# Windowed attention, forward and backward: mixing the tokens before the weight products, with two more DMA transposes and all loads on GpSimd

## Chip, cores, metric

One core of one Trainium2 chip. The metric is the device time of one execution in microseconds (us), lower is better.

## The reference, cut to what matters

The image is 256 x 256 tokens with C = 384 channels, in bf16. It is cut into 1024 windows of 8 x 8 = 64 tokens. The outputs are the forward result and the gradients for x, wqkv and wo.

```python
qkv = xw @ wqkv                       # xw: windows x 64 x 384
q, k, v = qkv[..., :C], qkv[..., C:2*C], qkv[..., 2*C:]
p = softmax(einsum('bqc,bkc->bqk', q, k) * C**-0.5)
o = einsum('bqk,bkc->bqc', p, v) @ wo
# out_0 = o; out_1, out_2, out_3 = gradients of x, wqkv, wo for a given grad_out
```

Both kernels fold the weights first: A = scale * Wq Wk^T and B = Wv Wo, with their transposes. With x the tokens of a window, g its grad_out, P the probabilities and dS the gradient of the scores:

- forward: P (x B), which equals (P x) B;
- gradient of x: dS (x A^T), which equals (dS x) A^T, plus dS^T (x A) and P^T (g B^T);
- weight gradients: x^T (dS x), and x^T (P^T g), which equals (P x)^T g.

The change rests on the equalities.

## The kernel before

The unit of work is a quad: four tiles of 128 tokens, each tile two windows. There are 128 quads, and one pass of the loop over them is called a step here. An eviction, below, copies a finished product out of PSUM, where PE leaves it. Work of three neighbouring quads is interleaved in a step: `a` is the next quad, `b` the current one, `c` the one before. Comments are mine.

```python
def load(st):                                        # three steps ahead
    for t in range(QUAD):
        nc.sync.dma_start(out=xq[:, t, :], in_=dram_tile(x, bp, t0 + t))            # SP
        nc.gpsimd.dma_start(out=dq[:, t, :], in_=dram_tile(grad_out, bp, t0 + t))   # GpSimd
def load_turn(st):                                   # tokens x channels -> channels x tokens
    for src, dst in ((dq, dT), (xq, xT)):
        nc.sync.dma_start_transpose(out=dst..., in_=src...)      # 12 blocks of 128x128 each
def to_tokens(st):                                   # the projections y = xA, z = gB^T turned back
    nc.sync.dma_start_transpose(out=tok..., in_=st["yz"]...)     # 24 blocks
def uv(st, t, part):                                 # u = x B (part 0), v = x A^T (part 1)
    for m in range(CK):                              # CK = 3
        nc.tensor.matmul(pj[:], lhsT=st["xT"][:, t, m, :], rhs=wgt[:, m, :], ...)
    cp(out=dst[:, t, :], in_=pj[:])                  # ACT, 8 of them a step
def store(dst, src, bp, t):                          # two DMAs of 64 tokens
    for h, w in ((LO, 1), (HI, 0)):
        nc.gpsimd.dma_start(out=dram_tile(dst, bp, t)[WIN * w:WIN * (w + 1)], in_=src[h, :])
def attend(st, pair, after=None):                    # 64x64 quarters of the PE array
    for t in pair:
        both((pu, "ST", "xq", True), (po, "PT", "uq", True))     # dS x,   P u
        ...                                                      # evict po -> store, pu -> Uq
        both((pw, "Pb", "dq", True), (pd, "ST", "vq", False))    # P^T g,  dS v
        ...                                                      # evict pw -> Wq
    ...                                              # close dx with tok, evict, store
# [...] in a step: scores(b), softmax(b) between the uv(b), project(a), weight gradients,
# attend(c, (2, 3)), attend(b, (0, 1)), to_tokens(a)
```

## Time and profile before

| | before |
|---|---|
| median of the first 3 runs | 2078.6 us (2078.22 to 2078.69) |
| PE (TensorE) busy | 2057.4 us, 99% of the span |
| DVE, ACT, POOL (GpSimd) busy | 67%, 71%, 68% |
| moved by DMA | 409.06 MB, mean 197 GB/s |

The page of before. After the busy times come two rows by 40 slices of the span in tenths (the clock that PE was granted, as a share of full speed, and the busy share of the DMA engines), then what the DMA queues moved (q1 is SP's queue, q0 GpSimd's; packets, MB, share of 16 engines' time), then the chain of waits that ended last.

```profile
...
PE 2057.4 (99%) x18814; PEld 1116.9 (54%) x18814; DVE 1391.1 (67%) x3235; ACT 1469.8 (71%) x3213; POOL 1418.0 (68%) x2566
...
PEclk9999999999999999999999999999999999999999
DMA  9999999999999999999999999999999999999992
...
DMA packets 997181, 409.06 MB, mean 197 GB/s; under 512 B 880704, under 2 KB 971584, under 8 KB 996928
...
q1 hardware_dynamic: 873648, 253.80, 72.1%
q0 software_dynamic: 122880, 151.68, 30.7%
...
PE 97%; DMA 2%; DVE 1%; ACT 0%; issue 0%
...
```

PE is busy throughout and is the chain. The DMA row is full too, but a share of busy packet time is not a limit by itself: the shares of the two queues add up to 103%, so time in which packets overlap is counted twice.

What SP does in one step (start in us, time to issue in us, operation, output<-input):

```profile
...
1011.19 3.96 SPq L156 DMA_TRANSPOSE tok<-yz  x1
1015.19 3.32 SPq L117 DMA_DIRECT2D xq<-in_x_dram  x4
1018.68 1.70 SPq L127 DMA_TRANSPOSE dT<-dq  x1
1020.42 2.26 SPq L127 DMA_TRANSPOSE xT<-xq  x1
1027.11 4.67 SPq L156 DMA_TRANSPOSE tok<-yz  x1
```

A step runs from one `tok` to the next: 1027.11 - 1011.19 = 15.92 us. SP is occupied for 3.96 + 3.32 + 1.70 + 2.26 = 11.2 us of it and then waits. From the chain of waits between 30 and 76 us (start, duration, what), the chain is DMA:

```profile
...
36.67 8.64 DMA tok<-yz
45.31 4.91 DMA dT<-dq
50.22 10.07 DMA tok<-yz
...
```

and this is what the engines and the DMA did between 32 and 75 us (length, then busy us of each engine with the number of instructions, granted clock, DMA share, GB/s):

```profile
...
32.00:75.00 43.00, 38.48 (x381) 19.59 (x380) 31.05 (x73) 34.62 (x78) 30.96 (x56) 1.00 1.16 218
...
```

### The profile page before, as it was taken

What the parts mean: (1) busy time and instruction counts of PE and PEld (TensorE: products, weight loads), DVE (VectorE), ACT (ScalarE), POOL (GpSimd) and SP (SyncE); (2) the same over time, 40 slices, a digit from 0 to 9 for tenths busy, and PEclk for the clock granted to TensorE, in tenths of its full rate; (3) what the DMA queues carried; (4) which work ended last, traced back from release to release, by engine and by line L of the source; (5) the groups of instructions that cost most, each with busy time, mean ns of one, the idle gap of its engine ahead of it and who ended that gap; (6) DMA issues with size and microseconds to landing.
All of it is one profiled execution on the core that took longest, in us unless ns stands there. A gap on an engine that the chain in (4) does not pass through costs nothing.

```text
span 2076.4 us, 51332 instructions
## 1 busy us (share of the span) xinstructions
PE 2057.4 (99%) x18814; PEld 1116.9 (54%) x18814; DVE 1391.1 (67%) x3235; ACT 1469.8 (71%) x3213; POOL 1418.0 (68%) x2566
## 2 busy tenths in 40 slices
PE   8999999999999999999999999999999999999998
PEld 4455555555555555555555555555555555555554
DVE  5666666666666666666666666666666666666665
ACT  5767777777777777777777777677777777777773
POOL 4766766767667767667676766676767677666764
PEclk9999999999999999999999999999999999999999
DMA  9999999999999999999999999999999999999992
GB/s 203 222 210 199 200 200 197 213 197 199 199 197 201 201 201 201 200 197 201 199 198 197 205 199 194 198 209 194 203 199 203 203 192 202 199 200 198 201 172 77
DMA packets 997181, 409.06 MB, mean 197 GB/s; under 512 B 880704, under 2 KB 971584, under 8 KB 996928
## 3 DMA queue, kind: packets, MB, share of 16 engines
q1 hardware_dynamic: 873648, 253.80, 72.1%
q0 software_dynamic: 122880, 151.68, 30.7%
q8 instruction: 147, 2.41, 0.5%
q14 instruction: 106, 0.87, 0.1%
q10 hardware_dynamic: 400, 0.29, 0.0%
HBM read 101.84 MB, written 101.84 MB: 98 GB/s over the span
## 4 chain that ended last, share of the span: by engine, by line
PE 97%; DMA 2%; DVE 1%; ACT 0%; issue 0%
PE pg L278 24%; PE pj L147 24%; PE pj L219 23%; PE pd L263 5%; PE pu L245 5%; PE sd L165 5%; PE pw L245 4%; PE pd L245 3%; PE pt L230 3%; DMA tok<-yz 1%; DMA dT<-dq 0%; PE pc L96 0%; DMA w_sb<-in_wqkv_dram 0%; PE pe L369 0%; PE po L245 0%; PE pt L74 0%
## 5 line engine op out<-in xcount | busy, mean ns | idle before, releaser
L235 POOL DMA_DIRECT2D out_dram<-osb x1024 | 576.2, 569 | 432.0 <-ACT osb L252 338.1
L235 POOL DMA_DIRECT2D out_dram<-dsb x1024 | 570.6, 563 | 133.9 <-DMA dq<-in_grad_out_dram 38.8
L280 DVE TENSOR_TENSOR GF_acc<-pg,GF_acc 128x384 f32<-128x384 f32 x258 | 144.0, 558 | 489.1 <-PE pg L278 489.1
L278 PEld LDWEIGHTS <-xq 128*128 128x128 bf16 x3072 | 300.3, 98 | 225.4 <-issue 0.9
L219 PEld LDWEIGHTS <-xT 128*128 128x128 bf16 x3072 | 291.8, 98 | 182.2
L252 ACT CAST osb<-po 128x384 bf16<-128x384 f32 x512 | 220.9, 483 | 233.5 <-PE pu L245 162.3
L219 PE MATMUL pj<-B_sb,xT 128*128 128x384 bf16 x1536 | 333.4, 326 | 0.0
L219 PE MATMUL pj<-AT_sb,xT 128*128 128x384 bf16 x1536 | 333.3, 326 | 0.0
L118 POOL DMA_DIRECT2D dq<-in_grad_out_dram x512 | 273.8, 549 | 71.6 <-PE pj L147 27.3
L221 ACT CAST uq<-pj 128x384 bf16<-128x384 f32 x512 | 247.3, 483 | 74.4 <-PE pj L219 70.1
L253 DVE CAST Uq<-pu 128x384 bf16<-128x384 f32 x512 | 280.6, 548 | 8.4 <-PE pu L245 8.4
L266 ACT CAST dsb<-pd 128x384 bf16<-128x384 f32 x512 | 220.7, 482 | 89.6 <-PE pd L263 68.5
L255 DVE CAST Wq<-pw 128x384 bf16<-128x384 f32 x512 | 280.6, 548 | 0.0
L147 PE MATMUL pj<-dT,BT_sb 128*128 128x512 bf16 x1152 | 269.6, 379 | 2.2 <-DMA dT<-dq 2.2
L147 PE MATMUL pj<-xT,A_sb 128*128 128x512 bf16 x1152 | 270.8, 380 | 0.0
L278 PE MATMUL pg<-Uq,xq 128*128 128x384 bf16 x1536 | 270.4, 326 | 0.0
L278 PE MATMUL pg<-Wq,xq 128*128 128x384 bf16 x1536 | 270.0, 326 | 0.0
L221 ACT CAST vq<-pj 128x384 bf16<-128x384 f32 x512 | 250.0, 488 | 2.4
L152 ACT CAST yz<-pj 128x512 bf16<-128x512 f32 x384 | 224.7, 585 | 16.8
L245 PE MATMUL pw<-dq,Pb 64*64 64x384 bf16 x1024 | 227.2, 329 | 0.2
L198 ACT COPY ps<-Pb 64x256 bf16<-64x256 bf16 x256 | 103.3, 403 | 149.8 <-DVE Pb L195 148.3
L245 PEld LDWEIGHTS <-ST 64*64 64x64 bf16 x2048 | 119.9, 105 | 161.6 <-issue 148.5
(65 smaller groups left out, 2501.6 us busy)
## 6 DMA issues: line engine op xcount, KB each, us to landing
xq<-in_x_dram SPq DMA_DIRECT2D x512, 96.0 KB, 4.0
dq<-in_grad_out_dram POOLq DMA_DIRECT2D x512, 96.0 KB, 5.3
out_dram<-osb POOLq DMA_DIRECT2D x1024, 48.0 KB, 4.1
out_dram<-dsb POOLq DMA_DIRECT2D x1024, 48.0 KB, 4.0
dT<-dq SPq DMA_TRANSPOSE x128, 6.3
xT<-xq SPq DMA_TRANSPOSE x128, 7.3
tok<-yz SPq DMA_TRANSPOSE x128, 8.0
w_sb<-in_wqkv_dram SPq DMA_DIRECT2D x1, 864.0 KB, 5.7
```

Of the source, the lines that this page charges most:

```text
L118: nc.gpsimd.dma_start(out=dq[:, t, :], in_=dram_tile(grad_out, bp, t0 + t))
L147: nc.tensor.matmul(pj[:].rearrange("p t w k -> p (t w k)"), lhsT=wgt[:, m, mo * P:(mo + 1) * P], rhs=src[:, :, m, :], start=(m == 0), stop ...
L152: ENG[EV["y"][mo]](out=yz[:, mo, :, 1:3, :], in_=pj[:])
L219: nc.tensor.matmul(pj[:], lhsT=st["xT"][:, t, m, :], rhs=wgt[:, m, :], start=(m == 0), stop=(m == CK - 1))
L221: cp(out=dst[:, t, :], in_=pj[:])
L235: nc.gpsimd.dma_start(out=dram_tile(dst, bp, t)[WIN * w:WIN * (w + 1)], in_=src[h, :])
L245: nc.tensor.matmul(dst[o, :], lhsT=st[lhs][h, t, :], rhs=st[rhs][h, t, :], start=True, stop=done)
L252: ENG[EV["o"][t]](out=osb[:], in_=po[:])
L253: ENG[EV["U"][t]](out=st["Uq"][:, t, :], in_=pu[:])
L255: ENG[EV["W"][t]](out=st["Wq"][:, t, :], in_=pw[:])
L266: ENG[EV["d"][t]](out=dsb[:], in_=pd[:])
L278: nc.tensor.matmul(pw[:], lhsT=st["xq"][:, t, ma * P:(ma + 1) * P], rhs=st["UW"[f] + "q"][:, t, :], start=(i == 0), stop=(i == n - 1))
```

## The change

The intent is to take work from PE, which is the limit. R = P x and U = dS x are made first, both are turned to channels x tokens by DMA, and then multiplied by B and A^T. The weight gradients use U and R directly. So the products P u, dS v and P^T g fall away. Each step's order has four stages instead of three. Stores become one DMA of 128 tokens, and the loads of x move from SP to GpSimd, which leaves SP to the transposes. Buffer counts and the last stage were rearranged as well. The core of the diff, with cuts marked [...]:

```diff
-            nc.sync.dma_start(out=xq[:, t, :], in_=dram_tile(x, bp, t0 + t))
-            nc.gpsimd.dma_start(out=dq[:, t, :], in_=dram_tile(grad_out, bp, t0 + t))
+            nc.gpsimd.dma_start(out=dq[:, t, :], in_=dram_tile(grad_out, bp, t0 + t))
+        for t in range(QUAD):
+            nc.gpsimd.dma_start(out=xq[:, t, :], in_=dram_tile(x, bp, t0 + t))
-    def uv(st, t, part):            [...]   # x B and x A^T, 24 matmuls of 128x384 a quad
-    def attend(st, pair, after=None): [...] # 32 quarter matmuls a quad
+    def mix(st, pair):                      # 16 quarter matmuls a quad
+        for t in pair:
+            for h, o in ((LO, HI), (HI, LO)):
+                nc.tensor.matmul(pR[h, :], lhsT=st["PT"][h, t, :], rhs=st["xq"][h, t, :], ...)
+                nc.tensor.matmul(pU[o, :], lhsT=st["ST"][h, t, :], rhs=st["xq"][h, t, :], ...)
+            nc.vector.tensor_copy(out=st["Rq"][:, t, :], in_=pR[:])
+            for h, o in ((LO, HI), (HI, LO)):
+                nc.scalar.copy(out=st["Uq"][h, t, :], in_=pU[o, :])
+    def out(st, pair): [...]                # po = R B   (12 matmuls of 128x384), evict, store
+    def dx(st, pair): [...]                 # pd = U A^T (12 matmuls of 128x384)
-        for h, w in ((LO, 1), (HI, 0)):
-            nc.gpsimd.dma_start(out=dram_tile(dst, bp, t)[WIN * w:WIN * (w + 1)], in_=src[h, :])
+        nc.gpsimd.dma_start(out=dram_tile(dst, bp, t0 + t), in_=src[:])
+        C_(to_channels, "Rq", "RT")         # in the step: a DMA transpose of 12 blocks
+        C_(to_channels, "Uq", "UT")         # and another
```

DMA transposes per step: xT 12, dT 12 and tok 24 blocks before; RT 12 and UT 12 more after, so 48 become 72.

## The prediction

> **What bounds it now.** The page shows TensorE busy 2057 of 2076 us (99%); the chain of waits is 97% PE and only 2% DMA. One step (one quad of windows) takes 15.92 us in the timeline, all of it PE: scores 0.7, U/V products 3.9, projections 2x1.95, weight-gradient products 2x2.05, two "attend" halves of 16 quadrant matmuls 2x1.0, turns 0.45, closing dx products 2x0.45. ACT (71%), DVE (67%) and POOL (68%) have slack. The DMA row is 9 in every slice, yet nothing waits for it in steady state. At the start it does: between 32 and 75 us the chain alternates between the waits for dT and tok, the SP queue issues without a pause, and its step there is 13.5 to 14.0 us. I read that as the old DMA-bound period, 13% below the PE's.
>
> **PE removed.** Products: 24 weight matmuls remain (as out and dx), but 32 quadrant matmuls per quad become 16: two mixes of about 0.5 us instead of two attends of 1.0. That is -1.0 us per step: 14.95 us, x128 = 1914, plus some 50 us of start and end: 1965 us if PE stayed the bound.
>
> **ACT, DVE, POOL.** ACT gives up 8 evictions (485 ns) and takes 8 half-height ones of the same length: about 11.5 us per step, still under the PE. DVE loses 4 x 548 ns. POOL issues 16 DMAs instead of 20 (0.56 us each): 9 us. The PSUM ring's waits, read in program order, fall on readers already done.
>
> **DMA added.** Two more DMA transposes per step (R and U, 12 blocks of 128x128 each): 48 blocks become 72, +50%. In bytes: 3.14 MB become 3.93 MB per step. The x loads leave SP for GpSimd, which saves SP about 2.6 us of issue; but the Trainium skill ("DMA: Bandwidth & Descriptors", section "Issuing engines are not separate DMA queues") says all queues end on the same 16 engines, so they go on costing. The trace agrees: transposes without other packets in flight move about 185 to 210 GB/s, and with any load or store beside them 105 to 150.
>
> Estimates of the new DMA-bound step:
> - bytes at the saturated start's 228 GB/s: 3.93/228 = 17.2 us;
> - SP occupation (mean dT 2.0, xT 2.9, tok 4.3): 4.3 + 4x2.7 = 15.1 us, before extra contention;
> - transpose rate of the steady state (9,216 packets at 580 per us): 15.9 us.
>
> So DMA takes over as the bound, at about 16.5 us: more than the old PE step. 16.5x128 + 50 = 2160 us.
>
> **Prediction.** 2160 us, 1990 to 2300. Faster by over 2%: 0.22; within 2%: 0.20; slower by over 2%: 0.58.
>
> **What would show it right.** PE busy falls to about 1930 us with idle time before out (waiting for RT), dx (UT), the projections (dT, xT) or the closing products (tok); SP transposes run back to back, RT and UT near 2.5 to 3 us of issue, landing 7 us or more; the chain carries a large DMA share; transposes take over 90% of the hardware queue. Mean bandwidth stays 200 to 240 GB/s.
>
> **What would make it wrong.** Full 128-token stores (16 engines instead of two halves) and fewer software DMAs might interfere less, so that a backlogged transpose queue reaches its unmixed rate: then the step is PE's 14.95 us and the kernel takes 1965. Or the loop RT landing -> out -> mix(2,3) -> eviction -> RT, about 6.5+1.3+7 us, adds waits of its own beyond my range.

## The result, and the profile after

The change made the kernel slower: 2372.11 us (2355.84 to 2388.91, 4 runs) against 2078.41 us (4 runs), ratio 1.1414 with a 95% interval of 1.1334 to 1.1494. A ratio is the mean time of one kernel's fast runs over that of the other's fast runs of the same rounds, so it is not quite the ratio of the medians that are quoted. The direction was forecast, the size was not: 2372 lies above the range of 1990 to 2300.

The page of the changed kernel, the same lines:

```profile
...
PE 2016.7 (85%) x16766; PEld 1047.4 (44%) x16766; DVE 1176.4 (50%) x2723; ACT 1488.9 (63%) x3213; POOL 1079.9 (46%) x2054
...
PEclk8899999999999998998999999999989999998999
DMA  9999999999999999999999999999999999999996
...
DMA packets 1300291, 508.82 MB, mean 214 GB/s; under 512 B 1232992, under 2 KB 1266528, under 8 KB 1300064
...
q1 hardware_dynamic: 1201360, 304.14, 82.1%
q0 software_dynamic: 98304, 201.46, 35.5%
...
PE 11%; DMA 6%; DVE 1%; SPq 0%; issue 0%; ACT 0%; DVEq 0%; ACTq 0%
...
```

PE is down to 85%, and this although its clock row shows slices at 8 (the mean granted clock is 0.94), so part of the busy time is slow time. The DMA moves 508.82 MB instead of 409.06 and runs at 214 GB/s instead of 197. The chain line adds up to 18% of the span only, so the chain could not be followed back far in this trace, and the waits below serve in its place.

What SP does in one step of it:

```profile
...
1016.10 8.86 SPq L138 DMA_TRANSPOSE tok<-yz  x1
1025.13 3.76 SPq L117 DMA_TRANSPOSE dT<-dq  x1
1029.12 1.54 SPq L117 DMA_TRANSPOSE xT<-xq  x1
1030.75 2.63 SPq L117 DMA_TRANSPOSE RT<-Rq  x1
1033.47 1.68 SPq L117 DMA_TRANSPOSE UT<-Uq  x1
1035.24 9.57 SPq L138 DMA_TRANSPOSE tok<-yz  x1
```

SP is issuing for 8.86 + 3.76 + 1.54 + 2.63 + 1.68 = 18.5 us of these 19.1. It no longer pauses before `tok`. The mean distance of two `tok` over some hundred steps is 18.2 us. Time to issue by transpose, minimum/median/maximum in ns, before and then after:

```profile
...
L127 SPq DMA_TRANSPOSE dT<-dq x128: 1463/1988/3095, 9.0 to 2002.2; - x128
L127 SPq DMA_TRANSPOSE xT<-xq x128: 1425/2886/4444, 10.9 to 2005.5; - x128
...
```

```profile
...
L156 SPq DMA_TRANSPOSE tok<-yz x128: 3632/4260/6755, 25.3 to 2029.9; - x128
...
```

```profile
...
L117 SPq DMA_TRANSPOSE dT<-dq x128: 1412/2900/6737, 7.7 to 2296.7; - x128
L117 SPq DMA_TRANSPOSE xT<-xq x128: 1413/3238/5926, 9.7 to 2298.6; - x128
L117 SPq DMA_TRANSPOSE RT<-Rq x128: 1423/2476/5532, 46.8 to 2338.1; - x128
L117 SPq DMA_TRANSPOSE UT<-Uq x128: 1451/2674/5224, 52.4 to 2339.9; - x128
...
```

```profile
...
L138 SPq DMA_TRANSPOSE tok<-yz x128: 4064/5790/9575, 30.0 to 2332.2; - x128
...
```

The minima stay alike and the medians grow: `tok` from 4.26 to 5.79 us, `dT` from 1.99 to 2.90 us. A `dT` takes up to 6.7 us to issue, where 1.4 us can do. I read a long issue time as the sign of a queue that is full, so that SP cannot hand on its work. The five medians sum to 17.1 us, nearly a step.

What PE waited for (engine, line, releaser, us in total, times, longest):

```profile
...
PE po L225 <- DMA RT<-Rq: 227.8, 91, 6.9
PE pj L129 <- DMA dT<-dq: 82.9, 40, 5.4
...
```

and one such wait in PE's timeline, with what comes behind it:

```profile
...
1016.27 1.23 PE L225 MATMUL po<-B_sb,RT 128*128 128x384 bf16 x6 [2.83 <-DMA RT<-Rq]
1017.29 3.75 PE L258 MATMUL pg<-Uq,xq 128*128 128x384 bf16 x12
...
1025.90 2.11 PE L258 MATMUL pg<-Uq,xq 128*128 128x384 bf16 x12
...
```

PE stood 2.83 us before `out`, for RT. The 12 matmuls behind it took 3.75 us, where the same 12 took 2.11 us nine microseconds later. That is the clock: over the 3.75 us the trace has a mean granted clock of 0.56, over the 2.11 us one of 1.00. The Trainium skill ("TensorE: Matmul & The Clock Gate", Part 1) says that an idle window of about 3.4 us puts PE to half its clock and a busy one releases it. This trace agrees in kind, though this wait was shorter: slow matmuls come right after it, and the clock row, all 9 in before, has some 8 here. I take the lower clock for a consequence of the waits; no run here held the clock fixed.

### The profile page after: what moved, and what is told of

Its sections match the earlier page's. It is cut to its first block, busy times and chain, and to the rows that moved or that the text cites. A ratio compares the mean times of both kernels' runs of the same rounds, so it can differ in the third digit from the quotient of the medians.

```text
span 2372.5 us, 45910 instructions
## 1 busy us (share of the span) xinstructions
PE 2016.7 (85%) x16766; PEld 1047.4 (44%) x16766; DVE 1176.4 (50%) x2723; ACT 1488.9 (63%) x3213; POOL 1079.9 (46%) x2054
## 2 busy tenths in 40 slices
DMA packets 1300291, 508.82 MB, mean 214 GB/s; under 512 B 1232992, under 2 KB 1266528, under 8 KB 1300064
## 5 line engine op out<-in xcount | busy, mean ns | idle before, releaser
L217 ACT CAST Uq<-pU 64x384 bf16<-64x384 f32 x1024 | 484.0, 473 | 290.2 <-PE pU L214 278.0
L221 POOL DMA_DIRECT2D out_dram<-dsb x512 | 269.5, 531 | 866.6 <-ACT dsb L246 831.2
L225 PE MATMUL po<-B_sb,RT 128*128 128x384 bf16 x1536 | 322.7, 351 | 248.2 <-DMA RT<-Rq 227.8
L215 DVE CAST Rq<-pR 128x384 bf16<-128x384 f32 x512 | 261.8, 553 | 371.3 <-PE pU L214 371.3
L221 POOL DMA_DIRECT2D out_dram<-osb x512 | 274.7, 539 | 243.5 <-ACT osb L232 93.9
L134 ACT CAST yz<-pj 128x512 bf16<-128x512 f32 x384 | 224.3, 585 | 224.5 <-PE pj L129 208.9
L113 POOL DMA_DIRECT2D xq<-in_x_dram x512 | 271.5, 552 | 125.9 <-DMA out_dram<-dsb 90.8
L225 PE MATMUL pd<-AT_sb,UT 128*128 128x384 bf16 x1536 | 291.5, 326 | 3.8 <-DMA UT<-Uq 3.2
L258 PE MATMUL pg<-dq,Rq 128*128 128x384 bf16 x1536 | 285.4, 338 | 0.0
L132 ACT CAST yz<-pj 128x512 bf16<-128x512 f32 x384 | 215.8, 592 | 84.9 <-PE pj L129 83.2
L258 PEld LDWEIGHTS <-Rq 128*128 128x128 bf16 x1536 | 155.8, 101 | 110.1 <-issue 17.2
## 6 DMA issues: line engine op xcount, KB each, us to landing
tok<-yz SPq DMA_TRANSPOSE x128, 11.2
```

What stands on the lines that cost most here:

```text
L113: nc.gpsimd.dma_start(out=xq[:, t, :], in_=dram_tile(x, bp, t0 + t))
L132: nc.scalar.copy(out=yz[:, mo, :, 0:4:3, :], in_=pj[:])
L134: nc.scalar.copy(out=yz[:, mo, :, 1:3, :], in_=pj[:])
L215: nc.vector.tensor_copy(out=st["Rq"][:, t, :], in_=pR[:])
L217: nc.scalar.copy(out=st["Uq"][h, t, :], in_=pU[o, :])
L221: nc.gpsimd.dma_start(out=dram_tile(dst, bp, t0 + t), in_=src[:])
```

## The experiments

Theory 1 was that the transposes, all on SP's queue, with the loads and stores that share the DMA with them, need more time in a step than PE. Theory 2 was that a loop of latencies sets the step: RT lands, then `out`, `mix`, eviction, and the next RT. Theory 3 was that moving the loads of x to GpSimd does the harm. Sixteen kernels were run. "After" and "before" in the expectations are the two kernels. In all runs the outputs were right except where the expectation says they are wrong. All times are medians; only a_ob8 has slow runs in it.

The results in one table. "Mean GB/s" and the MB are from each page's line of DMA packets. A step is taken from the distance of two `tok` in SP's timeline where the text gives one.

| run | what differs | us | ratio to before | MB moved | mean GB/s | PE busy |
|---|---|---|---|---|---|---|
| before | | 2078 to 2079 | 1 | 409.06 | 197 | 99% |
| after | | 2372.1 | 1.1414 | 508.82 | 214 | 85% |
| a_no_u | U not turned | 2199.8 | 1.0581 | 458.45 | 209 | 90% |
| a_no_r | R not turned | 2167.3 | 1.0425 | 458.45 | 211 | 90% |
| a_no_ru | neither turned | 1934.3 | 0.9307 | 408.08 | 211 | 98% |
| a_no_loads | no loads | 1972.2 | 0.9489 | 415.86 | 211 | 96% |
| a_no_x | no loads of x | 2167.3 | 1.0421 | 462.33 | 213 | 89% |
| a_no_stores | no stores | 2396.2 | 1.1529 | 414.27 | 174 | 85% |
| a_row_stores | tiny stores | 2125.9 | 1.0222 | 408.95 | 193 | 91% |
| a_x_on_sp | x loaded by SP | 2334.4 | 1.1225 | 508.80 | 218 | 85% |
| a_spread | loads of x spread | 2376.0 | 1.1420 | 508.82 | 214 | 85% |
| a_ob8 | 8 output buffers | 2373.8 | 1.1313 | 508.82 | 213 | 84% |
| b_plus_one | before + 1 transpose | 2158.8 | 1.0384 | 459.42 | 213 | 96% |
| b_plus_turns | before + 2 transposes | 2485.2 | 1.1954 | 509.77 | 205 | 88% |
| b_x_on_pool | before, x loaded by GpSimd | 2374.6 | 1.1393 | 409.09 | 172 | 91% |
| b_x_on_act | before, x loaded by ACT | 2311.4 | 1.1111 | 409.08 | 177 | 91% |
| b_x_pool_ob8 | b_x_on_pool, 8 output buffers | 2349.2 | 1.1303 | 409.08 | 174 | 91% |
| b_x_pool_o_sp | the same, out_0 stored by SP | 2090.4 | 1.0060 | 408.77 | 195 | 99% |

### The turns of R and U, taken away one at a time

```diff
-        C_(to_channels, "Uq", "UT")
-            apply(pd, st["UT"][:, t], AT_sb, False)
+            apply(pd, st["xT"][:, t], AT_sb, False)      # a_no_u; xT with 5 buffers
```

(`a_no_r` does the same to R and `out`, `a_no_ru` to both.)

> After, with the DMA transpose of U left out (dx reads xT in its place, a wrong result on purpose; all products stay). Theory 1, queue time: the SP queue's transposes are one after the other and their sum sets the step; 60 blocks instead of 72 at 506 packets per us make 15.2 us, about PE's own 15, so 2000 to 2090 us. Theory 2, loop: the chain RT landing, out, mix, eviction, RT sets the step and UT is not in it: it stays above 2250 us. Theory 3, loads on GpSimd collide with the transposes: a sixth of the collisions goes, about 2250 us.

> After, with the DMA transpose of R left out instead (out reads xT, wrong on purpose). Theory 1, queue time: the same as without U, 2000 to 2090 us, and the two within 3% of each other. Theory 2, loop: the loop is gone, so PE's own step of 15 us, about 1965 us, clearly below the run without U.

Measured: 2199.8 us without U and 2167.3 us without R. Each gives back half of the loss or more, and they are 1.5% apart. Theory 2 predicted a large difference, since only R is in the loop, and falls as the main cause. Theory 1 has the kind of the effect right but not its size: both lie above its 2090 us, because 506 transpose packets per us, the rate that I took from after, is not a constant. Over some hundred steps SP issues for 88% of the time without U and for 96% without R. PE waits 195 us for RT without U and 164 us for `dT` without R. Without U neither SP nor PE (90%) is full, so a rest of theory 2, the wait for RT to land, may be in that run's time; no run here settles it.

> After with neither R nor U turned (out and dx read xT, wrong on purpose; same products, same loads and stores). Shared budget: 3.15 MB a step at about 212 GB/s would need 14.8 us, so PE's own step of about 15 us: 1950 to 2020 us. This also checks the prediction's PE term of 14.95 us. If the pipeline of the new order has waits of its own (the loop being one, which is gone here too), it stays above 2080 us.

Measured: 1934.3 us. The PE and DMA lines of its page:

```profile
...
PE 1892.5 (98%) x16766; PEld 1021.8 (53%) x16766; DVE 1177.1 (61%) x2723; ACT 1467.5 (76%) x3213; POOL 1080.4 (56%) x2054
...
DMA packets 898878, 408.08 MB, mean 211 GB/s; under 512 B 831584, under 2 KB 865120, under 8 KB 898656
...
```

PE is the limit again at 98%. The mean step is 14.79 us, so the prediction's PE term of 14.95 us was right (the time is even 16 us below the expected range). SP issues for 76% of a step only. The new order has no waits of its own that matter.

### The same transposes added to the kernel before

```diff
+    def spare_turn(st):
+        for n in ("s0", "s1"):                           # b_plus_one: only "s0"
+            spare = qp.tile([P, QUAD, CK, P], BF16, tag="spare", name="spare")
+            nc.sync.dma_start_transpose(out=spare..., in_=st["xq"]...)
         B(attend, (0, 1))
+        B(spare_turn)
```

> Before, right result, with two more DMA transposes of 12 blocks in each step whose result nobody reads (the buffers of the last stage moved to make room). PE, ACT, DVE and the products are as before. Theory 1, queue time: the step becomes the queue's, 17 to 18.5 us, 2230 to 2420 us. Theory 2, loop: nobody waits for them, so 2080 to 2130 us.

Measured: 2485.2 us, slower than the changed kernel and 65 us above the range of theory 1, for two results that nobody reads. Its page:

```profile
...
PE 2187.0 (88%) x18814; PEld 1140.5 (46%) x18814; DVE 1390.7 (56%) x3235; ACT 1492.2 (60%) x3213; POOL 1417.4 (57%) x2566
...
DMA packets 1398623, 509.77 MB, mean 205 GB/s; under 512 B 1282144, under 2 KB 1373024, under 8 KB 1398368
...
```

Nothing of the new order, the mixing or the loads is in this kernel, so two more transposes a step are enough to cost as much as the whole change. This is the plainest evidence against theory 2.

> Before with one more DMA transpose a step instead of two: 3.54 MB a step. At 205 to 219 GB/s that is 16.2 to 17.3 us, above PE's 15.92: 2110 to 2260 us. If a threshold of another kind had been crossed with two, one costs nothing: 2078 to 2095 us.

Measured: 2158.8 us, inside the range of theory 1. The first extra transpose costs 80 us and the second 326 us. The first one meets slack, as I read it: SP is occupied for 11.2 of the old kernel's 15.92 us. But the second costs four times as much for the same bytes, and the mean rate drops from 213 to 205 GB/s. So the rate is not quite fixed; see below.

### Where do the loads and stores come in?

Theory 1 can be split: the transposes share one budget with all other traffic (1a), the transpose queue has a pace of its own whatever else moves (1b), or only the loads disturb the transposes (1c).

> After, with the loads of x back on the SP queue, as the kernel before has them. Theory 3, loads on GpSimd collide with transposes: 3% faster or more, below 2300 us, with fewer transposes meeting a load. Theory 1: the loads take the queue's time themselves (2.9 us of SP issue each step before), so no gain: 2340 to 2480 us.

Measured: 2334.4 us, a gain of 1.7% on after's ratio, between the two expectations. The rate rises to 218 GB/s with the same bytes. Theory 3 has at most a small part in this kernel.

```diff
+        if len(loaded) == 2 * GQ + 4:                    # a_no_loads: reuse the first ten quads
+            st["xq"], st["dq"] = loaded[0]
+            loaded.append(loaded.pop(0))
+            return
```

> After with loads only for the first ten quads, whose buffers are then used again in turn (wrong on purpose); all transposes and stores stay. Theory 1a, the transposes share one budget with loads and stores: 3.15 MB a step, 14.6 to 15.5 us, 1950 to 2060 us. Theory 1b, the transpose queue has its own pace, whatever else moves: still 2250 us or more.

Measured: 1972.2 us, and PE at 96%. All 72 blocks a step are still turned, and SP still issues for 97% of a step, but the step is 14.8 us and no longer 18.2. So the transposes have no fixed pace of their own (theory 1b), and they get through once other traffic makes way.

```diff
+        if bp < NBP - 1:                                 # a_no_stores
+            return
```

> After with out_0 and out_1 stored only for the last row of windows (the rest of the outputs is missing on purpose); all transposes and loads stay. Theory 1a: the same bytes go as without loads, so the same time within 3%. Theory 1b: 2250 us or more. If loads disturb the transposes more than stores do (they meet at 350 against 416 packets per us in the trace of after), it stays over 3% slower than the run without loads.

Measured: 2396.2 us, no gain at all from the same number of bytes, which seemed to speak for theory 1c. But the run is no fair test. This line of its waits shows why:

```profile
...
POOL dq L111 <- PE pg L260: 1312.7, 44, 61.2
...
```

Without stores GpSimd runs ahead until the loads find no free buffer, waits up to 61 us, and then issues the loads of three quads at once: 44 waits for 128 quads. The mean rate fell to 174 GB/s. The stores had paced the loads. So I ran it again with stores that wait as before but move one token:

```diff
-        nc.gpsimd.dma_start(out=dram_tile(dst, bp, t0 + t), in_=src[:])
+        nc.gpsimd.dma_start(out=dram_tile(dst, bp, t0 + t)[0, 0:1, :], in_=src[0:1, :])
```

> After with every store kept in its place and waiting as before, but moving only its first token (768 bytes instead of 96 KB; wrong on purpose). The run without stores was no test, because without them the loads ran ahead of the step and came in bursts of three quads; here GpSimd stays paced by the stores. Theory 1a, transposes share the engines with whatever else moves: half of the other bytes is gone, step 14.8 to 15.8 us, 1950 to 2080 us. Theory 1c, only loads disturb the transposes: 2250 us or more.

Measured: 2125.9 us. Stores do count: their bytes cost 2372 - 2126 = 246 us, so theory 1c falls. But it is 2% above the upper end of theory 1a, and it moves only 193 GB/s. With about the same bytes left, a_no_loads was 154 us quicker, so the loads weigh more here than the stores; why is not shown.

> After with the loads of grad_out kept and those of x left out after the first ten quads (wrong on purpose). A dose: between after (18.2 us a step) and no loads at all (14.8, PE's own). If the cost of a load is the time that it shares with transposes, about half of the way: 16 to 17 us, 2100 to 2220 us. If it is the burst of eight loads at the start of a step that does the harm, more than half: below 2080 us.

Measured: 2167.3 us, half of the way to no loads, as shared time predicts (though PE, at 96%, may cut off the far end of that way). It is the same gain as from leaving R unturned, for the same bytes (0.39 MB a step).

```diff
             nc.gpsimd.dma_start(out=dq[:, t, :], ...)
-        for t in range(QUAD):
-            nc.gpsimd.dma_start(out=xq[:, t, :], ...)
+        D_(dx_end, (0, 1))                               # a_spread, in the step
+        L_(load_x, (0, 1))
+        ...
+        L_(load_x, (2, 3))
```

> After, right result, with the four loads of x issued in two pairs in the middle of the step, between stores, instead of right behind those of grad_out. If the burst of eight loads at the start of a step does the harm: 2300 us or less. If the shared time does, whenever it falls: 2330 to 2420 us.

Measured: 2376.0 us. When in the step the loads come makes no difference, so the burst of eight is not the cause.

### The loads of x moved alone

> Before with only the loads of x moved to GpSimd, the part of the change that can be done alone. The bytes stay, 3.14 MB a step, and PE needs 15.92 us: 2078 to 2110 us, with fewer SP issues. If moving the loads is what costs (theory 3), 2140 us or more.

Measured: 2374.6 us. I had expected 2078 to 2110, and it is 265 us above that. Taken alone, this line of the change costs the old kernel as much as the whole change costs, yet undoing it in the changed kernel gives back 1.7%. Its bytes are those of before, and it moves only 172 GB/s, so its limit is another one. Four runs went into it.

> Before with the loads of x issued by ACT instead of SP. As in the run with them on GpSimd they now move beside the transposes, but they don't stand in GpSimd's queue, where a store waits for the landing of the DMA eight places before it. If that queue made the 14% of that run: 2080 to 2150 us. If the loads moving beside the transposes did: 2300 us or more.

Measured: 2311.4 us, which by its number speaks for the loads' company beside the transposes. But it is inconclusive: ACT itself was held up. Its timeline (ACTq is ACT issuing a DMA):

```profile
...
1009.85 4.64 ACTq L117 DMA_DIRECT2D xq<-in_x_dram  x3
1014.53 0.48 ACT L221 CAST uq<-pj 128x384 bf16<-128x384 f32 x1 [4.59 <-issue]
...
```

ACT was 4.64 us in issuing three loads while SP's `tok` and `dT` were under way, and its next eviction came 4.59 us late. A new wait had taken the place of the one I wanted to test.

> Before with the loads of x on GpSimd, as in the run that took 2375 us, and with 8 instead of 4 buffers for each kind of output tile (the buffers of the last stage moved to make room). If that run's 14% came from ACT waiting for an output buffer whose store stands behind the loads in GpSimd's queue (540 us of ACT's waits were for stores to land): 2080 to 2180 us. If it came from the loads moving beside the transposes: 2300 us or more.

```diff
-    ob = ctx.enter_context(tc.tile_pool(name="ob", bufs=4))
+    ob = ctx.enter_context(tc.tile_pool(name="ob", bufs=8))
```

Measured: 2349.2 us. Output buffers fall as the reason. In the waits of GpSimd (POOL) and of SP in this run:

```profile
...
POOL dq L118 <- DMA out_dram<-dsb: 133.0, 71, 4.4
POOL xq L117 <- DMA out_dram<-dsb: 121.8, 75, 5.2
...
```

```profile
...
SPq L127 <- DMA dq<-in_grad_out_dram: 864.3, 129, 10.9
...
```

SP waits 864 us for grad_out to land, because GpSimd issues it late. As built, each DMA on GpSimd waits for the landing of the one eight places before it: in this trace no DMA of GpSimd starts before that one has landed, while a quarter start before the one seven places back has. Of 2346 us GpSimd was busy issuing for 1681.8 us, and its waits for landings sum to 454 us. So its queue of 24 DMAs a step would be the limit. The test takes eight of them out:

```diff
-            nc.gpsimd.dma_start(out=dram_tile(dst, bp, t)[...], in_=src[h, :])
+            (nc.sync if dst is out_0 else nc.gpsimd).dma_start(out=dram_tile(dst, bp, t)[...], in_=src[h, :])
```

> Before with the loads of x on GpSimd and, in exchange, the stores of out_0 on SP (and 8 output buffers, as in the run that took 2349 us). The bytes stay and all eight loads still move beside the transposes, but GpSimd issues 16 DMAs a step instead of 24. If GpSimd's queue set the step of that run (24 issues of 0.56 us, 13.4 us, and about 4 us of waiting for a DMA eight places back to land): 2080 to 2160 us. If the loads' company beside the transposes did: 2300 us or more.

Measured: 2090.4 us, ratio 1.0060. The page shows PE as the limit again:

```profile
...
PE 2061.2 (99%) x18814; PEld 1118.8 (54%) x18814; DVE 1390.6 (66%) x3235; ACT 1464.4 (70%) x3213; POOL 1116.7 (53%) x2054
...
DMA packets 972638, 408.77 MB, mean 195 GB/s; under 512 B 856160, under 2 KB 947040, under 8 KB 972384
...
```

All loads on GpSimd cost this kernel 0.6% as long as GpSimd has 16 DMAs a step and not 24. The test also moves the bytes of out_0 to SP's queue, so it shows that GpSimd's queue was the limit, not that the number of DMAs is all that counts. The changed kernel has 16 because its stores are whole tiles. So the paradox is solved: in the old kernel the move fills GpSimd's queue, in the new one it does not, and the two losses of 14% have different causes.

> After with 8 instead of 4 buffers for each kind of output tile. If the bytes set the step (3.93 MB at 210 to 219 GB/s): within 2% of after, 2320 to 2420 us. If output buffers are the hidden wait here as well: 2280 us or less.

Measured: 2373.8 us, fast runs at a ratio of 1.1313 (1.1256 to 1.1370), within 1% of after's. Two of its four runs were slow; the fast ones took 2341.6 and 2362.1 us. No hidden wait for output buffers.

### What the runs say together

Leave out the runs at or close to PE's limit (before, a_no_ru, a_no_loads, b_x_pool_o_sp) and those held up by a queue, by ACT or by bursts (b_x_on_pool, b_x_on_act, b_x_pool_ob8, a_no_stores). Two runs stand on the border: b_plus_one, kept, and a_no_loads, left out, both have PE at 96% and SP issuing for 96 to 97% of the time. Of the ten that remain, nine move 205 to 218 GB/s on average while they carry 458 to 510 MB (a_no_loads, with 211 GB/s and 416 MB, would fit as well). 508.82 MB at 205 to 218 GB/s take 2334 to 2482 us, and the changed kernel took 2372. Packets fit less well than bytes: the ten run at 501 to 606 packets per us. Such a rate does not by itself show that the DMA is the limit, for a_no_ru moves 211 GB/s too, with PE as its limit. a_row_stores, at 193, is the exception: it lost 100 MB of stores, and its time fell by less than in proportion to its bytes. Single pieces differ as well: 0.39 MB a step (some 50 MB in all) cost 172 or 205 us as U's or R's transpose, 80 and 326 us as the first and second extra transpose in before, and 205 us as loads of x. The rate is good to some 5%, then, and is no law; why the second extra transpose costs so much is open.

To see what lies in the rate, I sorted the packet records of the traces into times with transpose packets (256 bytes) alone in flight, with load or store packets (512 bytes and more) alone, and with both, spreading each packet's bytes over its time. In the changed kernel transposes alone move 213 GB/s, plain packets alone 293, and in company 100 + 94 = 194, in 45% of the time. In before it is 205, 216 and 102 + 78 = 180, in 36% of the time. (The prediction had 185 to 210 alone and 105 to 150 in company.) If the two kinds simply took turns, their shares of the rates alone would add up to 100%. In the changed kernel they are 100/213 and 94/293, 79% in sum, so company costs about a fifth. (An expectation above has 350 and 416 transpose packets per us beside a load and a store; in this count it is 390 in company and 830 alone.) Why company costs that is not shown by any run here.

One question stays open: all transposes stand in SP's one queue, and no run issued them from elsewhere. So what SP's order costs, apart from what the DMA can carry in all, was not separated.

No version with right outputs beat the kernel before. The new order without its turns (1934 us) is quick, but turning R and U on PE instead would need 24 more transposes and 8 more evictions a step; I did not build it. Only half of the mixing would still move 458 MB, and the runs with those bytes (a_no_u, a_no_r, b_plus_one) took 2159 us or more.

## Why the prediction was wrong

- *"PE removed. ... -1.0 us per step: 14.95 us"*: right. a_no_ru ran at 14.79 us a step with PE at 98%.
- *"DMA takes over as the bound"*: right. Two extra transposes alone do it to the kernel before (2485 us), and taking them away restores PE as the limit (1934 us). That slower was the likelier side was therefore no luck.
- *"bytes at the saturated start's 228 GB/s: 3.93/228 = 17.2 us"*: the mis-sized term. I had divided the step's bytes by the distance of `tok` in three steps of the start. The window's own figure, 218 GB/s, was in the trace of before and would have given 18.0 us. The sustained rate after the change is 214, or 18.4 us; measured is 18.2. By the prediction's own sum (x128 + 50), 17.2 us make 2252 us and 18.0 us make 2354.
- *"at about 16.5 us"*: the step that failed. The measured step is 18.2 us. I put the answer below the byte estimate by weighing it against two lower ones. *"SP occupation ... 4.3 + 4x2.7 = 15.1 us"* took issue times from a kernel whose queue was not full. Issue times hold waiting too, and these grew to a sum of medians of 17.1 us. *"transpose rate of the steady state (9,216 packets at 580 per us): 15.9 us"* counted only the time with transposes in flight. While they were in flight the changed kernel kept 593 per us, but by the packet records they were in flight for 85% of the time, which makes 506 per us.
- *"Faster by over 2%: 0.22"*: too generous. It stood for transposes that reach their unmixed rate beside the new stores. They did not: they shared their time with loads or stores for 45% of the kernel, at less than half of their pace.
- *"RT and UT near 2.5 to 3 us of issue ... SP transposes run back to back ... Mean bandwidth stays 200 to 240 GB/s ... idle time before out"*: right (2.48 and 2.67 us; 18.5 of 19.1 us; 214 GB/s; 227.8 us for RT). *"landing 7 us or more"* holds for UT (7.0 us), not for RT (6.1), and the large DMA share of the chain could not be read.
- *"PE busy falls to about 1930 us"*: it is 2016.7 us. The same number of matmuls took 1892.5 us in a_no_ru at a clock of 0.99, against 0.94 here, so I put the difference down to the clock, which I had not thought of.
- *"The PSUM ring's waits ... fall on readers already done"*, *"ACT ... under the PE"*: right as far as a_no_ru shows; with neither turn, nothing else keeps PE from 98%.
- The loop of latencies, named as a risk, is not what sets the time: with R's turn or U's left out it is the same within 1.5%, and two turns outside any loop cost as much (2485 us).
- That the Trainium skill's "Issuing engines are not separate DMA queues" ("DMA: Bandwidth & Descriptors") makes moved loads go on costing was right for the changed kernel: on SP or on GpSimd they cost the same within 1.7%.

## What to carry to other kernels

When a kernel is limited by one engine, look at how near the next limit is before moving work to it, and measure that second limit as a sustained rate over bytes, from a stretch in which it really was the limit. Issue times and busy shares of a queue with slack say little about the same queue when it is full. And when one line of a change is tried alone in the old kernel, check that it meets the same neighbours there: the same loads on GpSimd cost 14% where they made 24 DMAs a step for it, and 1.7% or 0.6% where they made 16.

## What the Trainium skill lacked or had wrong

- "DMA: Bandwidth & Descriptors", "Latency and other measured facts", gives a DMA transpose 261 GB/s, or about 350 to 400 when contiguous. It has no figure for transposes beside ordinary loads and stores. Here transposes alone in flight moved 205 to 213 GB/s, the mix 180 to 194, and whole kernels with two or one more transposes a step 205 to 218.
- The same page, "Issuing engines are not separate DMA queues", says that issuing from several engines saves only the sequencer's time, "usually small relative to the DMA itself". In b_x_on_pool that time, with the wait for landings in GpSimd's queue, was the limit: 24 DMAs a step made 2349 to 2375 us, 16 made 2090 us with the same loads.
- The page does not say that an issuing engine can be held in an issue while other DMAs are under way. Here SP's issue of one `tok` took from 4.06 to 9.58 us, and ACT needed 4.64 us for three loads and evicted nothing in that time.
- "TensorE: Matmul & The Clock Gate", Part 1, puts the idle window at about 3.4 us. Here a PE wait of 2.83 us was followed by 12 matmuls in 3.75 us instead of 2.11, at a granted clock of 0.56, so a wait shorter than the window was enough. It is no single case: the trace has 49 stretches at half clock (the first 100 us and the last 60 us left out), and for 26 of them no idle time of PE that reaches into the 3.4 us before is as long as 3.4 us.
